# Linear attention and a two-layer network on one core: a new order table, and 16 warm-up matmuls in place of 22

## The chip, the cores and the metric

The kernel runs on one core of a Trainium2 chip. The metric is the device time of one execution in microseconds (us); the median of three runs of the kernel before is 908.88 us (907.92 to 911.11).

## What is computed

Performer attention for 8 batches, 8 heads, 576 positions and head width 64, with 128 random features, and behind it a network of 512 to 2048 to 512 on all 4608 positions, in float32:

```python
def phi(x):                       # x is q or k, scaled by 64 ** -0.25
    proj = np.einsum('bhsd,md->bhsm', x, omega)
    h = proj - np.sum(x * x, axis=-1, keepdims=True) / 2.0
    h = h - np.max(h, axis=-1, keepdims=True)
    return np.exp(h) / np.sqrt(m)
q_p, k_p = (phi(q_s), phi(k_s))
kv = np.einsum('bhsm,bhsd->bhmd', k_p, v)
z = np.sum(k_p, axis=2)
num = np.einsum('bhsm,bhmd->bhsd', q_p, kv)
den = np.einsum('bhsm,bhm->bhs', q_p, z)[..., None] + 1e-06
attn = num / den                  # then reshaped to (4608, 512)
h = x @ w_in
out = np.maximum(0.01 * h, h) @ w_out
```

## The kernel before

Positions are worked in nine blocks of 512. For every block the queries become features, the features are multiplied with the sums of their batch (128 x 65 numbers per head), and the block goes through the network. Numbers are split into a high and a low float16 part, so most products are three matmuls. Blocks 0 to 2 use plain products (L1489 up, L1511 down); from block 3 on the product up has Strassen's seven products (L1397), in the last two blocks the product down too (L1308).

**The first stretch**, which the change moves most, runs up to the first L1489 matmul. The features of batches 0 and 1 and of query block 0 are made in float32 from loads of whole heads: L831 loads q or k, L832 squares it on ScalarE, L858 projects it (32 matmuls to a head pair), L865 takes the maximum on VectorE, L886 subtracts it, L889 takes the exponential. For keys L980 sums features times values. For queries L1076 transposes on TensorE, L1079 takes the exponential, L1107 multiplies with the sums, and L1118 to L1121 divide; the result is split, turned by a DMA (L1033) and is the right operand of L1489.

At the same time the weights come in. L653 loads w_in in eight pieces of 1 MB (L655 the same for w_out) into four buffers, fix_big 88 to 91. Each piece is converted from 64-bit words by L667 (ScalarE), L670 (ScalarE) or L672 (VectorE), and L674; a buffer is free for the next piece when its readers are done. L681 sums squares of each piece on TensorE. When the eighth piece is in, L689 takes the maximum of the sums, L583 (two matmul records) spreads it over the partitions into a tile called scratch, and L587 to L597 on VectorE make the power of two by which all of w_in is scaled. Only then can the pieces be split into high and low parts (L547, L549, L700, L545, L555), and only then can L1489 begin.

The scratch tile is a part of the one PSUM bank "mi" into which L980 writes its sums as well:

```python
scratch = lambda: tiles["mi"][0][:, 384:]
```

**What sets the order.** Every piece of work is an operation with a number, one function that issues some instructions. ORDER is a list of all 3183 numbers; the instructions are issued in exactly that order, each on its engine, and ON names for the operations that can run on several engines which one it is. Nothing else decides the order: an engine works off its own part of the list, and so does SP with the DMAs. Waits between engines are put in where the tiles demand it, by the place in the list: an instruction that reads a tile waits for the writers of that tile that stand ahead of it.

Ahead of the list stand WARM_N matmuls on a constant tile (L1562 and the memset at L1570). Where the planner's own model sees a gap on TensorE, between() puts in further such matmuls of no use (L1562 again, on the identity).

```python
busy(tiles["ffn"][-1], WARM_N, blank)
for o in order:
    ...
    if o in fill and fill[o][0].place < len(tiles[fill[o][0].kind]):
        busy(at(fill[o][0]), fill[o][1], constant)
    o.run()
```

Of the kernel before, what the change touches and what calls it, by code (L numbers as in the profile page):

```python
# [62 lines left out]
WARM_N = 22  # L63
# [405 lines left out]
def performer_ffn(ctx: ExitStack, tc, qT, kT, qn, kn, vn, omT, eye, w_in, w_out, out):  # L469
# [1089 lines left out]
    def busy(bank, n, of):  # L1559

        for _ in range(n):
            nc.tensor.matmul(bank[:, :FILL_N], of[:, :P], of[:, :FILL_N], start=True, stop=True, skip_group_check=True)  # L1562
# [5 lines left out]
    with tc.manual_schedule():  # L1568
        blank = tiles["p32"][1].rearrange("p g m -> p (g m)").bitcast(F16)[:, :FILL_N]
        nc.gpsimd.memset(blank, 1.0)  # L1570
        busy(tiles["ffn"][-1], WARM_N, blank)
        for o in order:
# [53 lines left out]
```

## Time and profile before

| | |
|---|---|
| median of three runs | 908.88 us |
| the profiled execution's own time | 911.08 us |
| its span, first to last instruction | 909.2 us |
| TensorE (PE) busy | 893.3 us, 98% of the span |
| VectorE (DVE) busy | 739.5 us, 81% |
| ScalarE (ACT) busy | 533.3 us, 59% |
| GpSimd (POOL) busy | 378.3 us, 42% |
| mean granted TensorE clock | 0.996 of full speed |
| DMA | 145.91 MB, mean 160 GB/s |

The profile is one execution. Start times count from the first instruction. In the chain of waits each piece stands with its start, its length and what it was: work on an engine, the issue of a DMA (SPq), a DMA in flight, or "issue". In the timeline, the time in brackets is idle time of the engine before the piece, with what ended it. The granted clock is 1.00 at 2.4 GHz and 0.50 at 1.2 GHz.

### The profile page before, as it was taken

To read this page: it belongs to the slowest core of one execution; us is meant where nothing else is said; L and a number is where in the kernel's file an instruction comes from. 1 tells how busy PE (TensorE), PEld (TensorE's weight loads), DVE (VectorE), ACT (ScalarE), POOL (GpSimd) and SP (SyncE) were. 2 spreads that over 40 slices of the span, in tenths; PEclk is the share of its full clock that TensorE was granted. 3 is DMA by queue.
4 is the path that set the end of the run, shared out by engine and by line. 5 is a ranking of instruction groups with operands and counts; after the bars stand their busy time and mean duration, and the time that the engine had idled before them with its cause. 6 is when DMAs were issued, how large, how long until landed. Compare 5 with 4: busy or idle time off the path is not lost.

```text
span 909.2 us, 20952 instructions
## 1 busy us (share of the span) xinstructions
PE 893.3 (98%) x8513; PEld 609.6 (67%) x8513; DVE 739.5 (81%) x1372; ACT 533.3 (59%) x869; POOL 378.3 (42%) x325
## 2 busy tenths in 40 slices
PE   8989999999999999999999999999999999999998
PEld 6886645555555445587558855785578647888887
DVE  5978998778889887979999988889878996965644
ACT  5977778456563465577638874676544643542540
POOL 0141463325344543435623624566455614342511
PEclk9989999999999999999999999999999999999999
DMA  8968359464465669896889978497858744532401
GB/s 335 381 206 225 69 131 192 103 178 107 85 139 159 141 166 229 171 252 161 166 174 229 184 182 175 128 239 146 175 106 221 145 104 100 175 74 73 146 1 47
DMA packets 258784, 145.91 MB, mean 160 GB/s; under 512 B 191360, under 2 KB 238720, under 8 KB 257664
## 3 DMA queue, kind: packets, MB, share of 16 engines
q1 hardware_dynamic: 258688, 144.58, 66.1%
q8 instruction: 66, 1.08, 0.5%
q14 instruction: 30, 0.25, 0.1%
HBM read 81.36 MB, written 16.78 MB: 108 GB/s over the span
## 4 chain that ended last, share of the span: by engine, by line
PE 77%; DVE 15%; DMA 3%; ACT 2%; issue 1%; SPq 1%; DVEq 0%; ACTq 0%
PE fixps_ffn L1511 26%; PE fixps_ffn L1397 19%; PE fixps_ffn L1489 8%; PE lateps_ffn L1397 4%; PE attps_pj L779 4%; PE fixps_ffn L1308 4%; PE lateps_ffn L1308 4%; PE attps_mi L980 1%; DMA fix_row<-qT 1%; DVE proj_st L786 1%; PE attps_mi L1100 1%; DMA fix_big<-w_in 1%; DVE fix_big L555 1%; DVE fix_wt L674 1%; PE attps_mi L1102 1%
## 5 line engine op out<-in xcount | busy, mean ns | idle before, releaser
L1511 PE MATMUL fixps_ffn<-fix_wt,fix_big 128*128 128x512 f16 x1344 | 301.8, 379 | 0.0
L1511 PEld LDWEIGHTS <-fix_big 128*128 128x128 f16 x1344 | 127.1, 98 | 144.8
L1397 PEld LDWEIGHTS <-fix_wt 128*128 128x128 f16 x2016 | 194.6, 98 | 25.6 <-issue 0.5
L1397 PE MATMUL fixps_ffn<-fix_xt,fix_wt 128*128 128x256 f16 x1656 | 190.0, 273 | 0.2 <-DVE fix_row L545 0.2
L555 POOL TENSOR_TENSOR fix_big<-fix_row,fix_big 128x512 f16<-128x512 f32 x82 | 103.0, 1264 | 127.3 <-ACT fix_big L549 86.8
L1489 PE MATMUL fixps_ffn<-fix_xt,fix_wt 128*128 128x512 f16 x576 | 128.5, 379 | 0.0
L1489 PEld LDWEIGHTS <-fix_wt 128*128 128x128 f16 x576 | 54.9, 98 | 63.4
L808 ACT ACTIVATE att_p<-att_p,shift 128x1024 f32<-128x1024 f32 x52 | 59.4, 1142 | 57.3 <-DVE att_p L805 57.2
L555 POOL TENSOR_TENSOR att_ph<-att_p,att_ph 128x1024 f16<-128x1024 f32 x27 | 58.4, 2165 | 74.7 <-ACT att_ph L549 54.3
L786 DVE TENSOR_REDUCE proj_st<-attps_pj 128x8 f32<-128x1024 f32 (+1 forms) x68 | 72.8, 1074 | 11.1 <-PE attps_pj L779 10.8
L549 ACT ACTIVATE fix_big<-fix_row 128x512 f16<-128x512 f32 x108 | 65.7, 625 | 4.1 <-POOL fix_row L1150 1.7
L805 DVE SCALAR_TENSOR_TENSOR att_p<-attps_pj,proj_sc,proj_st 128x1024 f32<-128x1024 f32 x52 | 66.2, 1275 | 1.2
L763 DVE SCALAR_TENSOR_TENSOR proj_z<-proj_nat,proj_sc,proj_z 128x512 f16<-128x512 f32 (+1 forms) x52 | 47.7, 920 | 6.0 <-ACT proj_z L549 5.7
L779 PEld LDWEIGHTS <-proj_t 64*128 64x128 f16 x1416 | 39.7, 94 | 18.5 <-issue 16.9
L1412 DVE TENSOR_TENSOR fix_row<-fix_row,fixps_ffn 128x512 f32<-128x512 f32 x56 | 38.0, 681 | 16.8 <-PE fixps_ffn L1397 13.9
L1420 ACT ACTIVATE fix_row<-fix_row 128x512 f32<-128x512 f32 x69 | 42.6, 622 | 14.1 <-DVE fix_row L1412 14.1
L779 PE MATMUL attps_pj<-om,proj_t 64*128 64x128 f16 x1416 | 50.7, 217 | 0.0
L549 ACT ACTIVATE att_ph<-att_p 128x1024 f16<-128x1024 f32 x46 | 48.2, 1050 | 2.6 <-PE attps_mi L994 1.3
L549 ACT ACTIVATE fix_row<-fixps_ffn 128x512 f32<-128x512 f32 x47 | 27.8, 591 | 34.3 <-PE fixps_ffn L1397 20.5
L555 DVE TENSOR_TENSOR fix_big<-fix_row,fix_big 128x512 f16<-128x512 f32 x57 | 44.0, 775 | 3.6 <-ACT fix_big L549 3.4
L1494 ACT ACTIVATE fix_row<-fixps_ffn 128x512 f32<-128x512 f32 x48 | 28.0, 594 | 31.7 <-PE fixps_ffn L1489 27.4
L739 ACT ACTIVATE proj_z<-proj_nat 128x512 f32<-128x512 f32 (+1 forms) x56 | 36.0, 644 | 16.8 <-DMA proj_nat<-qn 11.2
(251 smaller groups left out, 1746.2 us busy)
## 6 DMA issues: line engine op xcount, KB each, us to landing
fix_wt<-w1s SPq DMA_DIRECT2D x38, 512.0 KB, 4.6
fix_wt<-w1s SPq DMA_DIRECT2D x38, 384.0 KB, 4.2
fix_v<-vn SPq DMA_DIRECT2D x16, 650.0 KB, 5.8
fix_big<-w_in SPq DMA_DIRECT2D x8, 1024.0 KB, 10.8
fix_big<-w_out SPq DMA_DIRECT2D x8, 1024.0 KB, 7.0
proj_nat<-qn SPq DMA_DIRECT2D x32, 256.0 KB, 3.4
out<-fix_row SPq DMA_DIRECT2D x32, 256.0 KB, 2.8
w1s<-fix_y SPq DMA_DIRECT2D x32, 128.0 KB, 2.5
```

The lines of the kernel that those rows point to most:

```text
L549: ("ACT", act(n, int(pointer)), lambda: nc.scalar.activation(dst(), src(), AF.Copy, scale=1.0 if scale is None else value()), False),
L555: o = ways([(e, c, lambda g=g: g.tensor_tensor(dst(), a(), b(), op=ALU.subtract), True) for e, c, g in (("POOL", pool_(n), nc.gpsimd), ("D ...
L763: op("DVE", stt(n) + 0.15, lambda: nc.vector.scalar_tensor_tensor(zl(), heads(), up(), zh(), op0=ALU.mult, op1=ALU.subtract), port=True, r ...
L779: nc.tensor.matmul(at(pj)[:, 512 * h + c * M:512 * h + (c + 1) * M], at(self.t)[r, 2 * (c0 + c) + x, :], om[r, w, :], start=(x + w == 0), ...
L786: op("DVE", dve(n * M), lambda: nc.vector.tensor_reduce(row(0), pv(), axis=AX.X, op=ALU.max), r=[pj], w=[st], prio=prio)
L805: op("DVE", dve(n * M), lambda: nc.vector.scalar_tensor_tensor(p(), pv(), down(), row(2).rearrange("p (g o) -> p g o", o=1).broadcast_to([ ...
L808: op("ACT", act(n * M, 1), lambda: nc.scalar.activation(flat(p()), flat(p()), AF.Exp, bias=shift), w=[p32], r=["ones"], prio=prio)
L1308: nc.tensor.matmul(o, ga(gp, f, 1)[:, 0, P * t:P * t + P], w(f, wp), start=(first and place + f % 2 + t + gp + wp == 0), stop=(place == 3 ...
L1397: nc.tensor.matmul(o, unit(at(wb[c]), u)[:, wp, P * a:P * a + P], mixes[j, c][n][1](xp), start=(first and a == 0 and i == 0), stop=(a == 1 ...
L1420: op("ACT", act(512), lambda: nc.scalar.activation(at(g), at(src), AF.Prelu, scale=H_DOWN_D if finish else H_DOWN_S, alpha=0.01), r=[src], ...
L1489: nc.tensor.matmul(at(ph), wk[wp][:, c:c + P], xt[:, xp, :], start=(k + wp + xp == 0), stop=(k == KT - 1 and wp == 1))
L1511: nc.tensor.matmul(at(po), part(f, gp)[:, t * P:(t + 1) * P], wf[wp], start=(n == 0 and f % 4 == 0 and gp == wp), stop=(n == 3 and f % 4 = ...
```

## The change

WARM_N goes from 22 to 16. ORDER, with the same 3183 operations, is another list, and ON gives 389 operations another engine: 108 go from GpSimd to VectorE, 101 from VectorE to GpSimd, 90 from ScalarE to VectorE and 90 from VectorE to ScalarE. No operation is added or left out; the useless matmuls that between() puts in become 72 in place of 61, since they follow from the list (59 in place of 52 ahead of the first L1489, 13 in place of 9 just behind its first products).

```diff
-WARM_N = 22
+WARM_N = 16
...
 ORDER = [
-    21, 0, 15, 30, 8, 7, 1, 131, 136, 41, 141, 59, 474, 22, 16, 2, 23, 3, 24, 27, 17, 25, 18, 4, 31, 10, 28, 26, 19,
...
 ON = {
...
     "POOL": [
-        40, 57, 75, 94, 111, 129, 178, 181, 189, 192, 242, 247, 271, 283, 291, 295, 299, 307, 311, 315, 319, 323, 361,
...
+        40, 57, 75, 111, 129, 178, 181, 189, 192, 242, 266, 275, 279, 287, 291, 295, 299, 303, 307, 311, 315, 323,
...
```

**SP, the first loads.** proj_nat and fix_row 92 to 95 are heads of q and k, fix_v 108 the values of batch 0, 109 those of batch 1 (650 KB to a row, two where it says x2), fix_big the 1 MB pieces of weights. Before:

```order
L831 DMA proj_nat_178<-kT 128x512
L902 DMA fix_v_108<-vn 128x1300 x2
L609 DMA ident<-eye 128x128
L653 DMA fix_big_88<-w_in 128x2048
L653 DMA fix_big_89<-w_in 128x2048
L831 DMA fix_row_93<-qT 128x512
L653 DMA fix_big_90<-w_in 128x2048
L831 DMA fix_row_94<-qT 128x512
L902 DMA fix_v_109<-vn 128x1300 x2
L653 DMA fix_big_91<-w_in 128x2048
```

Now:

```order
L831 DMA proj_nat_178<-kT 128x512
L609 DMA ident<-eye 128x128
L831 DMA fix_row_93<-qT 128x512
L902 DMA fix_v_108<-vn 128x1300
L831 DMA fix_row_94<-qT 128x512
L902 DMA fix_v_108<-vn 128x1300
L653 DMA fix_big_88<-w_in 128x2048
L653 DMA fix_big_89<-w_in 128x2048
L653 DMA fix_big_90<-w_in 128x2048
L831 DMA proj_nat_177<-kT 128x512
L653 DMA fix_big_91<-w_in 128x2048
```

The identity and the two query heads moved ahead of the weights; of the two halves of fix_v 109 one now stands between the sixth and the seventh piece of w_in and the other behind all eight, so that 650 KB less stand ahead of the eighth piece.

**PE, around the L583 matmul of w_in.** attps_mi 173 is the bank "mi", of which scratch is a part; fix_v and att_ph, fix_row are values and features of batch 1's sums (20 matmuls in four rows). Before:

```order
L858 MATMUL attps_pj_172<-fix_xt_98,fix_row_94 128x128 x2
L583 MATMUL attps_mi_173<-ident,mx_w_131 128x128
L980 MATMUL attps_mi_173<-fix_v_108,att_ph_161 128x65 x4
L980 MATMUL attps_mi_173<-fix_v_108,fix_row_97 128x65
L980 MATMUL attps_mi_173<-fix_v_108,att_ph_161 128x65 x4
L980 MATMUL attps_mi_173<-fix_v_108,fix_row_96 128x65
L1107 MATMUL fixps_ffn_113<-fix_kv_81,att_qp_164 128x65 x4
L980 MATMUL attps_mi_173<-fix_v_108,att_ph_162 128x65 x4
L980 MATMUL attps_mi_173<-fix_v_108,fix_row_97 128x65
```

Now:

```order
L858 MATMUL attps_pj_172<-fix_xt_98,fix_row_94 128x128 x2
L1107 MATMUL fixps_ffn_115<-fix_kv_81,att_qp_164 128x65 x4
L583 MATMUL attps_mi_173<-ident,mx_w_131 128x128
L980 MATMUL attps_mi_173<-fix_v_108,att_ph_161 128x65 x4
L980 MATMUL attps_mi_173<-fix_v_108,fix_row_96 128x65
L980 MATMUL attps_mi_173<-fix_v_108,att_ph_161 128x65 x4
L980 MATMUL attps_mi_173<-fix_v_108,fix_row_97 128x65
L1107 MATMUL fixps_ffn_114<-fix_kv_81,att_qp_164 128x65 x4
L980 MATMUL attps_mi_173<-fix_v_108,att_ph_162 128x65 x4
```

One L1107 group moved ahead of L583. What the rows don't show is the place in the list of VectorE's L587, which reads scratch: before it stood behind both groups of L980, now it stands behind the first and ahead of the second. On PE the two L1076 groups that came next, one before and one behind the next L858 group, now both stand behind that L858 group; and on VectorE one more operation, an L547 that takes 128x256 numbers out of "mi", stands between L587 and the L886 that later L1076 groups wait for.

**SP, the first transposed query features of block 1.** L1067 turns the high and the low part of a head pair's features; att_qp 163 is the first head pair, 164 the second. Before:

```order
L736 DMA proj_nat_178<-qn 128x4x128
L1067 DMA_TRANSPOSE att_qp_163<-att_ph_161 128x8x128 x2
L736 DMA proj_nat_177<-qn 128x4x128
L1067 DMA_TRANSPOSE att_qp_164<-att_ph_162 128x8x128 x2
L765 DMA_TRANSPOSE proj_t_181<-proj_z_180 128x8x128
```

Now:

```order
L736 DMA proj_nat_178<-qn 128x4x128
L1067 DMA_TRANSPOSE att_qp_163<-att_ph_161 128x8x128
L1067 DMA_TRANSPOSE att_qp_164<-att_ph_162 128x8x128
L1067 DMA_TRANSPOSE att_qp_163<-att_ph_161 128x8x128
L1067 DMA_TRANSPOSE att_qp_164<-att_ph_162 128x8x128
L736 DMA proj_nat_177<-qn 128x4x128
```

The second part of the first pair now stands behind the first part of the second pair.

## Rows read from the trace of the kernel before

**Rows 1.** The page, busy time of the engines.

```profile
PE 893.3 (98%) x8513; PEld 609.6 (67%) x8513; DVE 739.5 (81%) x1372; ACT 533.3 (59%) x869; POOL 378.3 (42%) x325
```

**Rows 2.** Busy time by stretch: up to the first L1489, and from there on.

```profile
0.00:72.10 72.10, 64.26 (x693) 58.20 (x694) 52.16 (x94) 53.81 (x70) 13.66 (x18) 0.95 0.86 305
72.10:905.00 832.90, 829.06 (x7822) 551.43 (x7819) 686.47 (x1278) 479.51 (x799) 364.62 (x307) 1.00 0.65 148
```

**Rows 3.** The chain of waits: start, length (us), what.

```profile
6.50 12.17 DMA fix_row<-qT
...
29.61 9.32 DMA fix_big<-w_in
...
43.12 1.99 PE attps_pj L858 x32
45.10 0.42 PE attps_mi L583 x2
45.52 2.18 PE attps_mi L980 x20
47.70 0.89 PE fixps_ffn L1107 x8
48.59 2.25 PE attps_mi L980 x20
...
63.66 3.72 PE attps_pj L858 x32
67.38 2.51 PE fixps_ffn L1107 x16
...
72.12 2.59 PE fixps_ffn L1489 x12
```

**Rows 4.** VectorE's timeline: start, length, what, idle time ahead of it.

```profile
22.54 0.68 DVE L672 TENSOR_SCALAR fix_wt<-fix_big 128x1024 uint32<-128x1024 uint32 x1
...
50.87 0.29 DVE L587 TENSOR_REDUCE pow_w<-attps_mi 128x1 f32<-128x128 f32 x1 [4.49 <-PE attps_mi L980]
...
57.73 0.42 DVE L1121 TENSOR_TENSOR fix_y<-fixps_ffn,att_r 128x256 f32<-128x256 f32 x1
...
59.32 1.22 DVE L886 TENSOR_TENSOR att_p<-attps_pj,proj_st 128x1024 f32<-128x1024 f32 x1
```

**Rows 5.** Busy time by stretch around 60 us; behind the counts granted clock, DMA share, GB/s.

```profile
50.00:62.50 12.50, 9.69 (x108) 8.65 (x107) 11.22 (x24) 10.55 (x15) 5.34 (x3) 0.97 0.88 293
62.50:67.50 5.00, 4.96 (x37) 4.40 (x38) 3.14 (x6) 4.93 (x7) 5.00 (x4) 0.50 0.77 148
67.50:72.10 4.60, 4.60 (x37) 4.56 (x38) 3.56 (x9) 2.93 (x3) 0.41 (x1) 0.89 1.12 283
```

**Rows 6.** The same view while the loads run; the last number is GB/s.

```profile
12.50:37.50 25.00, 22.89 (x281) 21.24 (x278) 21.27 (x40) 20.32 (x28) 0.00 (x0) 1.00 1.02 414
```

**Rows 7.** SP's timeline, three issues of w_in pieces that took 5.90 us.

```profile
24.04 5.90 SPq L653 DMA_DIRECT2D fix_big<-w_in  x3
```

**Rows 8.** PE's timeline.

```profile
1.10 4.88 PE L1562 MATMUL fixps_ffn<-att_p 128*128 128x256 f16 x22 [1.10 <-POOL att_p L1570]
5.90 2.62 PE L858 MATMUL attps_pj<-fix_xt,fix_row 64*128 64x128 f32 x32
...
53.10 0.66 PE L1076 MATMUL fixps_ffn<-ident,att_p 128*128 128x128 f32 x4 [1.38 <-DVE att_p L886]
...
75.01 1.14 PE L1562 MATMUL attps_pj<-ident 128*128 128x256 f16 x9
```

**Rows 9.** The page's costliest groups: busy us, mean ns of one.

```profile
L808 ACT ACTIVATE att_p<-att_p,shift 128x1024 f32<-128x1024 f32 x52 | 59.4, 1142 | 57.3 <-DVE att_p L805 57.2
...
L786 DVE TENSOR_REDUCE proj_st<-attps_pj 128x8 f32<-128x1024 f32 (+1 forms) x68 | 72.8, 1074 | 11.1 <-PE attps_pj L779 10.8
...
L805 DVE SCALAR_TENSOR_TENSOR att_p<-attps_pj,proj_sc,proj_st 128x1024 f32<-128x1024 f32 x52 | 66.2, 1275 | 1.2
...
L549 ACT ACTIVATE att_ph<-att_p 128x1024 f16<-128x1024 f32 x46 | 48.2, 1050 | 2.6 <-PE attps_mi L994 1.3
```

433 rows, old and new, of tables (ON, ORDER) are left out of this document.

## The prediction

> **What bounds the kernel now.** I read the page first: PE is busy for 893.3 us of a span of 909.2 [rows 1], so a change of order can only give back what is left, 15.9 us, and what runs at half clock. Then the busy times by stretch, to see where that lies [rows 2]. Behind the first L1489 matmul PE idles for 3.84 us of 832.90 (832.90 - 829.06) at a clock of 1.00; ahead of it for 7.84 us of 72.10, at a mean clock of 0.95. The rest lies at the ends. So the time is the start of L1489, 72.12 us [rows 3], and a packed 837 us behind it. The chain of waits for the start reads, in order of time: a query load that took 12.17 us from its issue at 6.50, since values and two pieces of weights stood ahead of it in the queue; the eighth piece of w_in, issued at 29.61 and landed at 38.93; some conversion; L583; two groups of L980 with an L1107 between them [rows 3]; and then VectorE's L587, which had been idle for 4.49 us and was let go by L980 [rows 4]. L587 needs only L583's result, which was there at 45.52; it waited until 50.87 because both L980 groups write the same bank and stand ahead of it in the list. After it VectorE works almost without a break (11.22 us of 12.50) while PE waits (9.69 us busy) [rows 5], until the L886 that ends at 60.54 [rows 4]. Then comes a stretch of PE at half clock: 0.50 for 62.50 to 67.50 [rows 5].
>
> **The change part by part.** All times are those of the profiled execution: 911.08 us with a span of 909.2. It lies 2.20 above the median of 908.88; I take the difference that the change makes from its rows and put it on the median.
>
> 1. *Loads.* From 12.5 to 37.5 us the queue moves 414 GB/s without a gap (DMA share 1.02) [rows 6]. Of what stood ahead of the eighth w_in piece, 650 KB (666 kB) now stand behind it: 666 / 414 = 1.6 us earlier, at 37.3. This is the end of the range for the good. The other end: the pieces 5 to 8 must wait for a free buffer, as three of them did on SP for 5.90 us [rows 7]. The buffer of the seventh is released by an L672 that ran at 22.54 [rows 4] and that now stands on VectorE behind divisions of the first query head. From its issue the eighth piece had 9.32 us [rows 3], so a release up to some 7 us later than 29.6 is hidden; if it were 10 us later, the last two megabytes would start some 10 us late and take 2 x 1049 / 414 = 5.1 us, a landing at about 40, 1.1 later than now. I take -1.6: the query loads that the divisions need are moved ahead of the weights too, and their 12.17 us shrink.
>
> 2. *L1107 ahead of L583.* One group of 8 is 0.89 us [rows 3]: +0.9.
>
> 3. *L587 no longer behind the second L980 group.* Between L583 and L587 now stands one group of L980 (2.18) on PE; the L1107 (0.89) and the second L980 (2.25) come later [rows 3]: -3.14. With 1 to 3, L587 starts at 50.87 - 1.6 + 0.9 - 3.1 = 47.0 in place of 50.87.
>
> 4. *VectorE from L587 to L886.* From 50.87 to 60.54 this is nearly solid work [rows 4, 5]; now it is the same operations in another sequence and one L547 of 128 x 256 numbers more; the nearest row is an L1121 of that size, 0.42 [rows 4]: +0.4. L886 then ends near 57.1. PE has waits to lose here as well: L1076 waited 1.38 us for L886 [rows 8]; now an L858 group of 1.99 [rows 3] stands ahead of it and covers that.
>
> 5. *The clock.* The half-clock stretch costs (1 - 0.97) x 12.50 + 0.50 x 5.00 + (1 - 0.89) x 4.60 = 3.4 us [rows 5], all on the path: behind L886 PE works without a break up to L1489, and there L858 took 3.72 in place of 1.99 and 16 L1107 matmuls 2.51 in place of 1.78 [rows 3]. It began after a stretch in which PE was busy 9.69 of 12.50 us [rows 5]. In the new order most of that idle time is gone, as VectorE is 3.5 us ahead and the transposes stand later. I take the whole 3.4 back; the other end is 0. The clock gate has a rule in the Trainium skill, in "TensorE: Matmul & The Clock Gate", section "HAM oscillation — how this bites in real kernels": PE keeps its full clock so long as no long idle gap interrupts it. By that rule gaps such as the 1.38 us of that stretch [rows 8] cost no clock, the half-clock stretch would have a cause that the new order leaves alone, and the sum would be without step 5: -3.0, 905.9 us. By the rows, in which the clock fell when small gaps had added up, it is -6.4. I go by the rows.
>
> 6. *Warm-up.* 22 matmuls took 4.88 us, 0.222 each [rows 8]: six fewer are 1.3 us. The first L858 came at 5.90 directly behind them [rows 8], so it can start up to 1.3 earlier. That is hidden: PE waits for loads afterwards, and the path runs through the eighth piece. I take 0; bounds -1.3 and, if the clock rises later for it, +1.3, hidden by the same loads. If the loads were no longer the bound, the whole 1.3 would count.
>
> 7. *Filling matmuls.* 13 in place of 9 behind the first L1489; 9 took about 1 us [rows 8]: +0.4. The 59 in place of 52 ahead of it stand in gaps of the loads: 0.
>
> 8. *The 389 operations on another engine, and the packed part.* DVE's and ACT's sums hardly move, as the exchanges are 108 against 101 and 90 against 90. What it does to the 3.84 us of PE idle [rows 2] the trace of before cannot show: between -1.9 (half of them go) and +6.4 (rival 2). I take 0, since before the packed part leaves the engines other than PE free for 17% and more of it (686.47 of 832.90 for VectorE) [rows 2].
>
> Sum: -1.6 + 0.9 - 3.1 + 0.4 - 3.4 + 0.4 = -6.4 us. L1489 starts at about 65.4, and 908.88 - 6.4 = **902.5 us**.
>
> **The rivals.**
>
> *1. The clock falls again.* Everything as above, but PE still waits ahead of the later L1076. From L583, now at 45.10 - 1.6 + 0.9 = 44.4, its work is 0.42 + 2.18 + 0.89 + 2.25 + 1.99 [rows 3], two L1076 of 0.66 [rows 8], another L858 and another L1107 of 1.99 and 0.89 [rows 3]: 11.9 us, to 56.3, and L886 ends at 57.1. That leaves a gap of 0.8 us, and more where ScalarE's exponentials come late. For it speaks that small gaps were enough before; against it, that PE idled 2.81 us of those 12.50 [rows 5], three times as much. The time is 902.5 + 3.4 = 905.9.
>
> *2. The gain before L1489 is given back behind it.* The packed part was idle for 3.84 us in 832.90 [rows 2]; a list with a new sequence of everything can have more. It decides from 6.4 us more, 10.2 in all, and the time is then 908.9, no change. Against it: VectorE, ScalarE and GpSimd have the same sums as before.
>
> *3. Slower: SP's transposes of block 1.* The second part of the first head pair's features now waits in SP's queue for the first part of the second pair. That part exists only after the second pair's maximum (L786 1.07), subtraction (L805 1.28), exponential (L808 1.14) and high part (L549 1.05) [rows 9], together 4.5 us, if they come after those of the first pair with nothing between. Where PE has no other work left, the num product waits that long, and a wait of that length can take the clock with it, 3.4 more by step 5: 7.9 us in all, and the time is 902.5 + 7.9 = 910.4. With the fall of the clock it decides from a wait of 3.0 us. Against it: PE has L1489 products to do meanwhile, and both pairs' projections stand close together.
>
> **How the numbers follow.** A measurement of this kernel can tell about 0.3%, 2.7 us, from no change: faster means below 906.15, slower above 911.6. My chances: forecast 0.55, rival 1 0.20, rival 2 0.15, rival 3 0.10. Rival 1 at 905.9 lies at the border, so half of it counts as faster, half as the same; nearly all of rival 2 is the same, with a little in either direction; of rival 3 six parts in ten are slower. Faster: 0.55 + 0.10 + 0.01 = 0.66; slower: 0.06 + 0.01 = 0.07; same: the rest, 0.27. The range starts at 898.5: the forecast with half the packed idle gone (-1.9), a warm-up that counts (-1.3) and rounding. It goes up to 909.8, over the late loads (+2.7), rival 1 and rival 2, and leaves out most of rival 3 and a little below. The likeliest case alone reaches from 899 to 905.2 (late loads).
>
> **What would show it.** In the changed profile L587 for w_in should start near 47 and show an idle time of 2 to 3 us before it, ended by L980; the eighth w_in piece should land near 37.3; the granted clock should be 1.00 from 12.5 us on, with no 0.50 stretch between 50 and 70; the first L1489 should start near 65.4. PE's idle time behind it should be 2 to 6 us. The query load that took 12.17 us should take 4 to 6. If L1489 starts near 69 with a half-clock stretch ahead of it, rival 1 holds; if it starts near 65 and the span is still 905 or more, rival 2 or 3, told apart by whether PE's waits for att_qp exceed 3 us in one place. The prediction is wrong if L587 still waits until 50 or later, or if the eighth piece lands after 39.

## The result, and the profile after

The changed kernel takes **915.06 us** (914.12 to 917.76, five runs) against 909.53 (907.92 to 911.11) for the kernel before, measured beside it. The ratio is 1.0066, with an interval of 1.0044 to 1.0088: slower by 0.7%. The forecast was 902.5, faster. The profiled execution took 914.36 with a span of 912.4, that is 3.2 more than the span of before.

The page, busy time of the engines after [rows 1]:

```profile
PE 892.0 (98%) x8518; PEld 607.5 (67%) x8518; DVE 757.4 (83%) x1379; ACT 536.2 (59%) x869; POOL 368.9 (40%) x318
```

Busy time by stretch after [rows 2, 5, 6]:

```profile
0.00:72.10 72.10, 67.01 (x745) 59.68 (x745) 60.04 (x102) 57.00 (x71) 14.81 (x19) 1.00 0.85 304
72.10:905.00 832.90, 821.56 (x7746) 545.00 (x7745) 696.28 (x1276) 478.49 (x797) 354.13 (x299) 1.00 0.65 148
12.50:37.50 25.00, 24.91 (x301) 23.01 (x300) 23.36 (x41) 20.68 (x25) 0.00 (x0) 1.00 1.02 413
50.00:62.50 12.50, 10.14 (x123) 9.07 (x121) 12.14 (x19) 10.07 (x15) 7.46 (x5) 1.00 0.51 174
62.50:67.50 5.00, 5.00 (x39) 3.98 (x38) 4.66 (x11) 4.74 (x6) 4.41 (x4) 1.00 0.62 207
```

PE's and VectorE's timelines after [rows 3, 4, 8]:

```profile
50.93 0.66 PE L1076 MATMUL fixps_ffn<-ident,att_p 128*128 128x128 f32 x4
53.83 0.66 PE L1076 MATMUL fixps_ffn<-ident,att_p 128*128 128x128 f32 x4 [2.25 <-DVE fix_y L1121]
...
65.59 2.75 PE L1489 MATMUL fixps_ffn<-fix_xt,fix_wt 128*128 128x512 f16 x12
68.18 1.58 PE L1562 MATMUL fixps_ffn<-ident 128*128 128x256 f16 x13
```

```profile
45.92 0.29 DVE L587 TENSOR_REDUCE pow_w<-attps_mi 128x1 f32<-128x128 f32 x1 [2.26 <-PE attps_mi L980]
...
53.37 0.41 DVE L1121 TENSOR_TENSOR fix_y<-fixps_ffn,att_r 128x256 f32<-128x256 f32 x1
```

The first stretch came out almost as forecast: L1489 starts at 65.59 us instead of 72.12, the half-clock stretch before it is gone (1.00 from 62.5 to 67.5, where before had 0.50), and L587 starts at 45.92 after 2.26 us of idle time. It is behind L1489 that the time went. PE's idle time there is 832.90 - 821.56 = 11.34 us, where before had 3.84 [rows 2]. The longest of PE's waits from 72 to 905 us (in total, times, longest); first those of before, then those of after:

```profile
PE attps_mi L1102 <- DMA att_qp<-att_ph: 1.2, 2, 0.8
PE attps_pj L858 <- ACT att_p L802: 0.9, 1, 0.9
PE attps_mi L1100 <- DVE fix_x L1121: 0.6, 1, 0.6
```

```profile
PE fixps_ffn L1511 <- DVE fix_row L1412: 1.7, 1, 1.7
PE attps_mi L1102 <- DMA att_qp<-att_ph: 1.6, 2, 1.1
PE attps_pj L779 <- DMA proj_t<-proj_z: 1.5, 3, 0.6
PE fixps_ffn L1397 <- DMA fix_xt<-fix_xn: 1.4, 1, 1.4
PE attps_mi L992 <- DVE proj_st L791: 1.0, 1, 1.0
```

No wait is long; there are more of them, for VectorE and for transposes by DMA.

**The lag table.** To see where a kernel gains or loses, the two traces are laid side by side at equal work of PE: each matmul counts with the spacing that its kind has when nothing waits (0.216 us for a 128x512 product of L1489 or L1511, 0.109 for L1397, and so on; filling matmuls count zero), and the lag is the difference in time at which the same sum is reached. The reference is the profiled execution of before (911.08, some 2 us above its median), so that much of a gain belongs to the reference. A minus means earlier than before. The columns are times in the trace of before.

```
                          79   111   189   204   360   391   437   468   593   623   881
after                   -5.9  -5.6  -6.7  -5.3  -6.4  -2.1  -0.5  +1.1  +1.5  +3.1  +3.5
after, 22 warm-ups      -5.8  -5.5  -6.6  -5.6  -6.9  -4.8  -1.7  -1.0  -0.6  +1.4  +1.9
new to 347, then old    -5.7  -5.4  -0.2  -0.2  -0.7  -0.7  -0.4  -0.4  -0.4  -0.4  -0.1
old to 347, then new    -1.1  -1.1  -2.2  +0.8  -0.5  +0.9  +3.0  +4.2  +4.6  +7.4  +8.1
new to 510, then old    -4.8  -4.5  -6.0  -6.0  -7.0  -7.0  -6.6  -6.6  -6.6  -6.6  -6.7
new to 1014, then old   -4.6  -4.3  -5.4  -1.1  -1.9  -1.9  -1.9  -1.9  -1.2  -1.2  -1.1
read of L587 alone      -5.1  -5.1  -5.2  -5.2  -5.8  -5.8  -5.8  -5.8  -5.0  -5.0  -5.0
```

After is 6 us ahead from 80 to 360 us and then gives up 10 us, 4 of them between 375 and 391.

**The place at 384 us.** SP's waits and timeline of after, and busy time by stretch:

```profile
SPq L736 <- DVE proj_z L763: 5.4, 1, 5.4
```

```profile
373.51 0.39 SPq L736 DMA_DIRECT2D proj_nat<-qn  x1
...
376.21 5.61 SPq L1033 DMA_TRANSPOSE fix_xt<-fix_xn  x2
```

```profile
380.00:384.00 4.00, 1.94 (x42) 1.51 (x41) 3.88 (x4) 2.40 (x5) 0.00 (x0) 1.00 1.12 248
384.00:388.00 4.00, 4.00 (x40) 2.90 (x39) 3.97 (x7) 1.43 (x3) 2.12 (x1) 0.57 1.09 183
```

SP waits 5.4 us to issue a query load (L736, operation 1501), because VectorE still reads its buffer. Behind it in SP's queue stand the two L1033 transposes that L1397 needs. PE idles for 2.06 of 4.00 us, and then the granted clock is 0.57 for 4 us, another 0.43 x 4 = 1.7 us.

**The place at 421 us.** Timelines of VectorE, GpSimd and PE of after:

```profile
418.65 1.12 DVE L791 SCALAR_TENSOR_TENSOR proj_st<-proj_st,proj_sc,proj_sq 128x8 f32<-128x8 f32 x1
419.80 2.04 DVE L796 SCALAR_TENSOR_TENSOR proj_st<-proj_sq,proj_st 128x8 f32<-128x8 f32 x1
...
422.13 0.68 DVE L1412 TENSOR_TENSOR fix_row<-fix_row,fixps_ffn 128x512 f32<-128x512 f32 x1
```

```profile
417.60 2.14 POOL L555 TENSOR_TENSOR fix_big<-fix_row,fix_big 128x512 f16<-128x512 f32 x1
419.70 2.12 POOL L555 TENSOR_TENSOR att_ph<-att_p,att_ph 128x1024 f16<-128x1024 f32 x1
```

```profile
422.86 1.46 PE L1511 MATMUL fixps_ffn<-fix_wt,fix_big 128*128 128x512 f16 x6 [1.71 <-DVE fix_row L1412]
```

Two operations on 128 x 8 numbers take 1.12 and 2.04 us. They end at 419.77 and 421.84, and GpSimd's two operations end at 419.74 and 421.82: each of VectorE's ended with the one of GpSimd that had started ahead of it. L1412 stands behind them, and PE waits 1.71 us for L1412. The groups of these two lines, before and after (total, mean ns), first before:

```profile
L791 DVE SCALAR_TENSOR_TENSOR proj_st<-proj_st,proj_sc,proj_sq 128x8 f32<-128x8 f32 (+1 forms) x68 | 27.5, 404 | 0.4
L796 DVE SCALAR_TENSOR_TENSOR proj_st<-proj_sq,proj_st 128x8 f32<-128x8 f32 x52 | 15.2, 293 | 1.8
```

```profile
L791 DVE SCALAR_TENSOR_TENSOR proj_st<-proj_st,proj_sc,proj_sq 128x8 f32<-128x8 f32 (+1 forms) x68 | 34.3, 504 | 0.5
L796 DVE SCALAR_TENSOR_TENSOR proj_st<-proj_sq,proj_st 128x8 f32<-128x8 f32 x52 | 21.0, 403 | 1.8
```

The same operations take 12.6 us more in all (34.3 + 21.0 against 27.5 + 15.2), since more of them fall beside GpSimd's: of the 120, 32 take over 0.5 us in after and 19 in before, and every one of these ends 0.02 to 0.03 us behind a GpSimd operation that had started ahead of it. VectorE's busy time as a whole grew by 17.9 us, from 739.5 [rows 1] to 757.4.

### The profile page after: what moved, and what is told of

The parts are those of the page before. It is cut to its first block, busy times and chain, and to the rows that moved or that the text cites. A ratio compares the mean times of both kernels' runs of the same rounds, so it can differ in the third digit from the quotient of the medians.

```text
span 912.4 us, 20980 instructions
## 1 busy us (share of the span) xinstructions
PE 892.0 (98%) x8518; PEld 607.5 (67%) x8518; DVE 757.4 (83%) x1379; ACT 536.2 (59%) x869; POOL 368.9 (40%) x318
## 4 chain that ended last, share of the span: by engine, by line
PE 73%; DVE 17%; DMA 4%; issue 2%; ACT 2%; POOL 1%; SPq 1%; DVEq 0%; ACTq 0%; POOLq 0%
PE fixps_ffn L1511 24%; PE fixps_ffn L1397 14%; PE fixps_ffn L1489 8%; PE lateps_ffn L1397 5%; PE lateps_ffn L1308 5%; PE attps_pj L779 4%; PE fixps_ffn L1308 3%; PE attps_mi L980 2%; DMA att_qp<-att_ph 1%; DVE proj_z L763 1%; PE attps_pj L858 1%; DVE fix_big L555 1%; DVE fix_wt L674 1%; DVE att_p L805 1%; PE attps_mi L1100 1%
## 5 line engine op out<-in xcount | busy, mean ns | idle before, releaser
L1511 PE MATMUL fixps_ffn<-fix_wt,fix_big 128*128 128x512 f16 x1344 | 301.6, 379 | 1.7 <-DVE fix_row L1412 1.7
L1511 PEld LDWEIGHTS <-fix_big 128*128 128x128 f16 x1344 | 127.2, 98 | 147.3 <-issue 1.9
L1397 PEld LDWEIGHTS <-fix_wt 128*128 128x128 f16 x2016 | 194.7, 98 | 28.5 <-issue 2.6
L1397 PE MATMUL fixps_ffn<-fix_xt,fix_wt 128*128 128x256 f16 x1608 | 186.5, 273 | 2.0 <-DMA fix_xt<-fix_xn 1.4
L555 POOL TENSOR_TENSOR fix_big<-fix_row,fix_big 128x512 f16<-128x512 f32 x86 | 107.9, 1265 | 137.7 <-ACT fix_big L549 72.8
L1489 PE MATMUL fixps_ffn<-fix_xt,fix_wt 128*128 128x512 f16 x576 | 128.6, 379 | 0.0
L555 POOL TENSOR_TENSOR att_ph<-att_p,att_ph 128x1024 f16<-128x1024 f32 x33 | 71.5, 2169 | 78.9 <-ACT att_ph L549 62.6
L1489 PEld LDWEIGHTS <-fix_wt 128*128 128x128 f16 x576 | 54.9, 98 | 63.0
L549 ACT ACTIVATE fix_big<-fix_row 128x512 f16<-128x512 f32 x111 | 67.5, 623 | 6.1 <-DVE fix_row L1150 4.1
L1412 DVE TENSOR_TENSOR fix_row<-fix_row,fixps_ffn 128x512 f32<-128x512 f32 x57 | 38.6, 682 | 19.1 <-PE fixps_ffn L1397 15.7
L763 DVE SCALAR_TENSOR_TENSOR proj_z<-proj_nat,proj_sc,proj_z 128x512 f16<-128x512 f32 (+1 forms) x52 | 51.0, 983 | 2.9 <-ACT proj_z L549 2.7
L549 ACT ACTIVATE att_ph<-att_p 128x1024 f16<-128x1024 f32 x49 | 51.2, 1049 | 3.5 <-PE attps_mi L980 2.9
L555 DVE TENSOR_TENSOR fix_big<-fix_row,fix_big 128x512 f16<-128x512 f32 x56 | 45.2, 809 | 5.7 <-ACT fix_big L549 5.6
L549 ACT ACTIVATE fix_row<-fixps_ffn 128x512 f32<-128x512 f32 x45 | 26.7, 593 | 38.8 <-PE fixps_ffn L1397 31.9
L1397 PE MATMUL lateps_ffn<-fix_xt,fix_wt 128*128 128x256 f16 x408 | 47.8, 273 | 0.0
```

Of the source, the lines that this page charges most:

```text
L549: ("ACT", act(n, int(pointer)), lambda: nc.scalar.activation(dst(), src(), AF.Copy, scale=1.0 if scale is None else value()), False),
L555: o = ways([(e, c, lambda g=g: g.tensor_tensor(dst(), a(), b(), op=ALU.subtract), True) for e, c, g in (("POOL", pool_(n), nc.gpsimd), ("D ...
L763: op("DVE", stt(n) + 0.15, lambda: nc.vector.scalar_tensor_tensor(zl(), heads(), up(), zh(), op0=ALU.mult, op1=ALU.subtract), port=True, r ...
L1397: nc.tensor.matmul(o, unit(at(wb[c]), u)[:, wp, P * a:P * a + P], mixes[j, c][n][1](xp), start=(first and a == 0 and i == 0), stop=(a == 1 ...
L1489: nc.tensor.matmul(at(ph), wk[wp][:, c:c + P], xt[:, xp, :], start=(k + wp + xp == 0), stop=(k == KT - 1 and wp == 1))
L1511: nc.tensor.matmul(at(po), part(f, gp)[:, t * P:(t + 1) * P], wf[wp], start=(n == 0 and f % 4 == 0 and gp == wp), stop=(n == 3 and f % 4 = ...
```

## The experiments

Kernels with longer tables have their lines 6 to 8 further down: L590 or L591 there is L583, L1084 is L1076. Before was measured beside each set; its medians were 908.8 to 909.4, with single runs from 905 to 917. The ratio is to before in the same set, with its interval; it comes from the single runs, so it is not always the quotient of the two medians. The edits of the lists are written in short.

**The two halves apart.** NEW and OLD are the two tables; each operation runs on the engine of the table from which its place comes.

```diff
-ORDER = NEW
+ORDER = NEW[:347] + [n for n in OLD if n not in NEW[:347]]
```

> The first 347 operations of the new list with their new engines and 16 warm-up matmuls, and behind them all others in the order and on the engines of the list before. Theory A (the new list gains about 6 us ahead of the first L1489 and loses about 10 us in the packed part, independently of each other): L1489 starts near 66, PE idles behind it for about 4 us as before, and the time is 3 to 6 us below the kernel before (904 to 906.5 against 909.5). Rival B (the loss is the price of the head: work that arrives 6 us earlier collides with loads and buffers later on): the time is above the kernel before, near 913 to 915, with waits of PE behind 350 us.

Measured: 911.12, ratio 1.0022 (1.0006 to 1.0038).

```diff
-ORDER = NEW
+ORDER = OLD[:347] + [n for n in NEW if n not in OLD[:347]]
-WARM_N = 16
+WARM_N = 22
```

> The mirror image: the first 347 operations and 22 warm-up matmuls of the kernel before, and behind them the new list and its engines. Theory A: L1489 starts near 72 as before, PE idles behind it for some 11 us, and the time is 9 to 10 us above the kernel before (918 to 920). Rival B: no more than 3 us above the kernel before (912 or less), since the head that causes the loss is gone.

Measured: 919.16, ratio 1.0114 (1.0079 to 1.0150). The new list behind entry 347 loses 9 us by itself (-1.1 to +8.1 in the lag table), as it does in after (-5.9 to +3.5). The first half failed to show its gain: the lag is -5.4 at 111 us and -0.2 at 189. PE's timeline there:

```profile
117.33 0.49 PE L590 MATMUL attps_mi<-ident,mx_v 128*128 128x128 f32 x2 [2.82 <-DVE fix_kv L1015]
117.66 1.76 PE L1569 MATMUL attps_pj<-ident 128*128 128x256 f16 x9
```

It is the joint: L583 waits 2.82 us for VectorE, the clock is at half for 3.4 us behind it (118.0 to 121.4), and the planner has put filling matmuls there. So it was done once more without the 13 fillers behind the joint:

```diff
-    fill = between(order)
+    fill = {o: f for o, f in between(order).items() if order.index(o) < 347}
```

> The first 347 entries of the new list and the rest of the old one, as in the run that took 911.1, without the 13 filling matmuls at 118 to 137 us (1.4 us, some of them at half clock). Theory (what was lost at the joint is a wait of 2.8 us for VectorE, the clock's fall behind it and these fillers): 909, between 908 and 910, the wait and the fall still there. Rival (the fillers keep the clock up and cost nothing): 911 to 912.

Measured: 909.35, ratio 1.0011 (0.9997 to 1.0025). By the ratios that is some 1 us less than with them, with intervals that overlap. The wait there was 1.4, without a fall of the clock, and behind the joint the lag stays: -2.5 at 189 us, -2.2 at the end. A splice has a cost at its joint, and the joint has to be chosen.

**The splice further on.**

```diff
+ORDER = NEW[:1014] + [n for n in OLD if n not in NEW[:1014]]
```

> The first 1014 entries of the new list with the new engines (some 295 us of the span), the rest of the old list with the old engines; 16 warm-ups. Theory A (the new first stretch gains some 6 us, the new list's packed part loses some 9, nearly all of it behind 360 us): 903.5, between 902 and 905.5, PE's lag against before about -6 from 80 us to the end. Rival (a lead is given back whatever list follows, since loads and VectorE set the pace of the packed part, as behind the joint of the run with 347 entries): 908 to 911, with the lag back at 0 within some 100 us of the joint.

Measured: 909.34, ratio 0.9992 (0.9968 to 1.0017). Busy time by stretch:

```profile
190.00:197.70 7.70, 5.76 (x33) 2.45 (x31) 7.63 (x12) 3.58 (x7) 5.82 (x5) 1.00 1.07 177
197.70:201.10 3.40, 3.08 (x16) 1.42 (x17) 2.54 (x7) 0.60 (x1) 0.94 (x1) 0.51 1.06 259
```

The lead goes in one place, 190 to 201 us: PE idles 1.94 us for query transposes (L1067) and the clock falls. In after's trace the first of these transposes is issued at 187.7 us, behind a v load and a weight load, and lands at 194.5, 6.8 us later (before: 199.5 to 203.1, 3.6); the same place cost 1.3 there. So the splice was put ahead of it:

```diff
+ORDER = NEW[:510] + [n for n in OLD if n not in NEW[:510]]
```

> The first 510 entries of the new list with the new engines (some 146 us of the span, so past the new first stretch and ahead of the query transposes near 190 us), the rest of the old list with the old engines; 16 warm-ups. Theory A (the new first stretch gains 6 us, and the places near 195, 384, 421 and 460 us, which all lie behind entry 510 of the new list, give it back): 904, between 902.5 and 905.5, with a lag against before of -5 to -6.5 us that stays to the end. Rival (the packed part gives a lead back whatever list follows): 908 to 911, with the lag back near 0 behind 200 us.

Measured: **904.48**, ratio 0.9948 (0.9923 to 0.9972): faster than both kernels. PE's waits from 72 us on are down to

```profile
PE attps_mi L591 <- DVE mx_w L697: 0.8, 1, 0.8
```

and smaller ones. The packed part keeps a lead when its list is the old one. The loss is the new list, with its engines, behind entry 510.

**Order or engines.** 389 operations change engine. Behind entry 347 all got their old engine back, with the new order:

```diff
-ON = NEW_ON
+ON = {operation: (NEW_ON if operation in NEW[:347] else OLD_ON)}
```

> The new list whole; behind its entry 347 every operation on the engine that it had before. Theory E1 (the loss of the packed part comes from the moves between VectorE, ScalarE and GpSimd): 907 to 910, the stalls behind 380 us gone. Theory E2 (it comes from the order of the entries, SP's above all): 914 to 917, with the stall of L1397 near 384 us still there.

Measured: 984.83, ratio 1.0831 (1.0795 to 1.0868). That decides for neither theory: PE has 635 matmuls more, fillers that the planner put in where it foresaw waits. Without them behind entry 347:

> The new list whole with the old engines behind entry 347, as in the run that took 985, but without the filling matmuls behind entry 347: the planner had put 635 of them there, since it foresaw waits (69 us at 0.109 each). Theory E2 (the order makes the waits, the engines little): 915 to 922. Theory E1 (the engine moves make them, the old engines take them away): 906 to 910. If the old engines fit the new order worse than the new ones: over 922.

Measured: 950.40, ratio 1.0456 (1.0429 to 1.0484). PE's line of the page, with and without those fillers:

```profile
PE 959.7 (98%) x9153; PEld 668.6 (68%) x9153; DVE 762.9 (78%) x1373; ACT 533.1 (54%) x868; POOL 377.3 (38%) x325
```

```profile
PE 905.2 (95%) x8518; PEld 613.2 (65%) x8518; DVE 759.1 (80%) x1373; ACT 532.5 (56%) x868; POOL 378.4 (40%) x325
```

So to take the engine moves back doesn't mend the new order, it makes it 35 us worse. The old order with the new engines was not run. Order and engines are one plan, and half of it can't be judged alone: how the loss divides between them stays open.

**Mending the new list.**

```diff
-..., 1501, 1699, ..., 1193, ..., 1195, ..., 1196, ..., 1701, ...
+..., 1193, 1501, ..., 1195, 1196, 1699, 1701, ...
```

> The changed kernel with one place of SP's queue in another order: the two L1033 transposes of block 4 ahead of a query load that waits for its buffer and of a load of values (and the L912 that reads these behind them). Theory C (at 383.8 us PE waited for these transposes for 1.4 us because they stood in SP's queue behind the load, and the wait took the clock with it, 3.4 us of half speed costing half of that or more): the wait of L1397 for fix_xt and the half-clock stretch at 384 us are gone, and the time is about 3 us below the changed kernel (912 against 915). Rival: the transposes were late for the work that makes their input; then the wait stays and the time is that of the changed kernel, 915.

Measured: 922.66, ratio 1.0139 (1.0113 to 1.0166). The edit made a worse wait, as VectorE's timeline and PE's show:

```profile
384.61 1.49 DVE L920 TENSOR_REDUCE mx_v<-fix_v 128x1 f32<-128x1280 f32 x1 [7.77 <-DMA fix_v<-vn]
```

```profile
389.82 1.47 PE L787 MATMUL attps_pj<-om,proj_t 64*128 64x128 f16 x24 [5.49 <-DVE att_p L813]
```

The v loads that it put later are awaited by VectorE, which stood still for 7.77 us. Next, operation 1193 alone:

```diff
-..., 1501, 1699, 1463, 1193, ...
+..., 1193, 1501, 1699, 1463, ...
```

> The new list with one entry moved: operation 1193 (an L1033 transpose of block 4) ahead of operation 1501 (an L736 query load that waits for its buffer) on SP; the v loads stay where they are, unlike the run that moved them too. Theory C (the wait of 1.4 us of L1397 at 384 us and the clock's fall behind it come from this transpose standing behind 1501): 912, between 910.5 and 913.5, no half-clock stretch near 385 us. Rival (the other transposes' turn on the queue or the engines sets it): 914.5 to 916.

Measured: 916.07, ratio 1.0065 (1.0038 to 1.0092). At its place it did what was meant: between 375 and 391 us the loss is 1.6, not 4.0, with no half clock. But in the profiled execution the place at 195 us, where the list is after's, took 4.0 in place of 1.3 (1.9 of waits and half clock from 196 us for 3.4), and the median did not fall. Six moves at once:

```diff
+1193 ahead of 1501
+999, 421 behind 779, 780, 805
+2274, 1972 behind 2211, 2212
+1510 behind 1291
```

> The new list whole, with six entries moved: 1193 (L1033 transpose) ahead of 1501 (query load); the loads 999 (v) and 421 (L1164) behind the query transposes 779, 780 and 805; the weight loads 2274 and 1972 behind the query transposes 2211 and 2212; VectorE's 1510 (the small operations of L797's helper) behind 1291 (L1412). Theory N (the loss of the packed part is the sum of these named waits: 1.3 near 195 us, 4.0 near 384, 1.9 near 421, 1.3 near 611): 907, between 905.5 and 909. Rival (there is no slack in the new list's packed part: what is mended at one place is lost at another): 912.5 to 917.

Measured: 914.33, ratio 1.0058 (1.0028 to 1.0087). Up to 593 us the lag is 4.4 better than after's (-2.9 against +1.5); then PE waits for one of the weight loads that were moved, and the clock falls:

```profile
609.08 3.17 PE L1405 MATMUL fixps_ffn<-fix_xt,fix_wt 128*128 128x256 f16 x14 [2.27 <-DMA fix_wt<-w1s]
```

Without the third line of that diff:

> The new list whole with four of the six moves of the earlier mending: 1193 ahead of 1501; 999 and 421 behind 780 and 805; 1510 behind 1291. The weight loads 2274 and 1972 stay where the new list has them (in the run with all six, PE's lag was 4.3 us better than the new kernel's up to 592 us, and the product behind those two loads then waited 2.4 us at 607 with a half-clock stretch, 4 us lost). Theory N (the waits are places that can be mended one by one, and moving those two loads was itself the mistake): 911, between 909.5 and 912.5, with the lag at 592 us kept to 640 but for some 1.3 us. Rival (the packed part has no slack: any mending is lost elsewhere): 913 to 917.

Measured: 912.77, ratio 1.0040 (1.0028 to 1.0053), between the two ranges. PE's timeline of this run:

```profile
382.48 0.34 PE L787 MATMUL attps_pj<-om,proj_t 64*128 64x128 f16 x6 [0.74 <-DMA proj_t<-proj_z]
...
425.70 1.47 PE L1405 MATMUL fixps_ffn<-fix_xt,fix_wt 128*128 128x256 f16 x12 [0.49 <-DVE fix_row L1420]
```

Where after waited 1.4 and 1.7 us there are 0.74 and 0.49. And the same without its 9 fillers behind entry 347:

> The new list with the four moves (1193, 999, 421, 1510), without the 9 filling matmuls that the planner had put behind entry 347 (some 1.0 us at 381 and 435). Theory N with fillers as the part that hid it: 911.5, between 910.5 and 912.3. If the fillers lay in waits that are there anyway: 912.8, as with them.

Measured: 912.13, ratio 1.0037 (1.0020 to 1.0053), which can't be told from 912.77. So waits can be mended one by one, but other waits remain or take their place: four moves meant for some 7 us give 2 to 3 by the ratios, and the intervals of these still overlap with that of after (1.0044 to 1.0088). From 80 us to the end the first of the two kernels loses 6.9 us in its profile (-5.3 to +1.6) and the second 6.0 (-1.8 to +4.2), not 9.4.

**The read of L587 alone**, on the old list: operation 173 (L587 to L597) directly behind 172 (L583), ahead of both L980 groups (83, 90).

```diff
-172, 83, 68, 90, 71, 98, 173, 99,
+172, 173, 83, 68, 90, 71, 98, 99,
```

> The kernel before with one operation moved: the read of w_in's maximum (L587 to L597 on VectorE) directly behind its L583 in the list, so that it waits for neither group of L980. Theory D (step 3 of the prediction: both groups write the bank that L587 reads, and the wait for them sits on the path to the first L1489): L587 starts near 45.6 in place of 50.9, L1489 3 to 5 us earlier than 72.1, and if the half-clock stretch goes as well up to 7; the time is 2 to 5 us below the kernel before. Rival E (VectorE's wait was hidden; the loads and PE's own work set the start): L1489 within 1 us of 72 and the time unchanged.

Measured: 906.07, ratio 0.9957 (0.9941 to 0.9973). VectorE's timeline, and busy time by stretch:

```profile
45.39 0.29 DVE L593 TENSOR_REDUCE pow_w<-attps_mi 128x1 f32<-128x128 f32 x1 [0.67 <-PE attps_mi L589]
```

```profile
62.50:67.50 5.00, 5.00 (x42) 4.41 (x43) 4.45 (x10) 4.79 (x5) 1.71 (x3) 1.00 1.13 266
```

L587 (here L593) starts 5.5 us earlier, released by L583 and no longer by L980, and the half-clock stretch is gone from this trace. One moved entry gives 3.3 of the 4.5 us that the best splice gives.

**The loads and the warm-ups.** The old list with that read, the new order of the first loads and 16 warm-ups, then the same with 22:

```diff
+1, 41, 7, 59, 8 behind 30; 473 behind 113; 475 behind 82; 477 behind 484
+173 behind 172
```

> The old list and engines with the new order of the first loads, with operation 173 directly behind 172, and with 16 warm-ups. Theory D plus step 1 (the loads are worth 1.6 to 4 us beside the 3.3 of the read): 904, between 902 and 905. Rival (what the loads gain ahead of 25 us is waited out at the next load, so that the read alone counts): 906, between 905.3 and 907.

Measured: 906.98, ratio 0.9975 (0.9951 to 0.9999).

> The old list and engines with the new order of the first loads, with operation 173 directly behind 172, and with 22 warm-ups (as the earlier run with 16, and nothing else changed). If the warm-ups count for the clock in the first 25 us (the run with 16 had 6.8 us at half clock there, the one with the read alone and 22 had 3.4): 904, between 902.5 and 905.5. If they do not: 906.5, between 905.5 and 908.

Measured: 908.23, ratio 0.9996 (0.9967 to 1.0024). Both miss their better case: on the old list the loads add nothing to the read alone that can be seen in the time, and 22 warm-ups are no better than 16. (In the trace of the second the lag is -6.4 at 79 us, 1.3 better than with the read alone; 3.0 of it go at 147 us, where L1102 waits 1.7 us and the clock falls. In the first the clock is at half from 19.5 to 26.3 us. Ten of its twelve runs have a mean clock of 0.994 to 0.996 and took 906.7 to 910.7 us; the two with 0.999 took 903.8 and 903.9. So the loads may be worth what was expected where the clock holds, but two runs don't show it.) With the new list:

> The new list whole, with 22 warm-ups in place of 16. Step 6 of the forecast (the warm-ups cost nothing, since they end ahead of the first load's landing): 915, as with 16, between 914 and 916. Rival (fewer or more of them change when the clock is granted or delay the first product): over 1.5 us away from 915 on either side.

Measured: 914.11, ratio 1.0054 (1.0029 to 1.0080), the same as with 16. This trace is the best witness against the clock as the main cause: it has no half-clock stretch ahead of 910 us, and still loses from -5.8 to +1.9. PE's timeline of it:

```profile
382.61 1.14 PE L1405 MATMUL fixps_ffn<-fix_xt,fix_wt 128*128 128x256 f16 x9 [1.46 <-DMA fix_xt<-fix_xn]
...
388.61 0.20 PE L1108 MATMUL attps_mi<-fix_kv,att_qp 128*128 128x65 f16 x1 [1.36 <-DMA att_qp<-att_ph]
```

**What is left of the first stretch.** On the best splice, the L1121 operations ahead of the scalings of the weights:

```diff
-72, 176, 90, 91, 73, ...
+72, 73, 176, 90, 91, ...
-69, 174, 180, ..., 116, 70,
+69, 70, 174, 180, ..., 116,
```

> The run with the first 510 entries of the new list, with two entries moved: 73 (L1121) directly behind 72, and 70 (L1121) directly behind 69, both L1120, on VectorE, so ahead of the weight scalings 174, 180, 176 and 175. Theory (the 2.25 us for which PE's L1076 waits at 51 us for L1121, which stands behind some 4 us of scalings on VectorE, go): 902.3, between 901 and 903.5. Rival (the scalings, later by as much, are awaited next, by L1489): 904 to 905, as without the edit.

Measured: 905.57, ratio 0.9960 (0.9945 to 0.9974), no gain. The wait for L1121 is gone, and its size stands at the next L1076:

```profile
56.98 1.97 PE L1084 MATMUL fixps_ffn<-ident,att_p 128*128 128x128 f32 x8 [2.27 <-DVE att_p L894]
```

VectorE works without a break there; to move an operation ahead moves another one back.

## Why the prediction was wrong, step by step

**Steps 1 to 5 and 7 were right in sum.** Together they said that L1489 would start near 65.4; in after's trace it started at 65.59, 6.5 us earlier. The splice at entry 510 shows 4.5 us of that in the time (904.48); before's trace, from which the 6.5 are taken, lay 2.2 above its median. The sum was met in part by luck, since steps 1 to 3 gave more and step 4 less than forecast.

- *Step 1 (loads, -1.6).* The last piece of w_in landed at 36.2 in place of 38.93, so -2.7, by SP's rows of after (issued at 27.1, 9.1 to its landing):

```profile
L653 SPq DMA_DIRECT2D fix_big<-w_in x2: 328/328/328, 25.6 to 27.1; - x2
...
DMA to landing us min/median/max: 8.1/8.6/9.1
```

- *Steps 2 and 3 (L587 near 47.0).* 45.92, and the idle time ahead of it 2.26 in place of 4.49. The read alone shows step 3 by itself.
- *Step 4 (VectorE to L1489, L1076 covered).* Failed: the same operations did not take the same time, and L1076 was not covered. One L547 took 2.56 us, where the other eight of its size on w_in and w_out in both traces took 0.72 to 0.75. GpSimd's L555 had started 0.12 us ahead of it:

```profile
50.49 2.56 DVE L547 TENSOR_SCALAR fix_wt<-fix_wt,pow_w 128x1024 f32<-128x1024 f32 x1
```

```profile
50.37 2.13 POOL L555 TENSOR_TENSOR fix_wt<-fix_wt,fix_wt 128x1024 f16<-128x1024 f32 x1 [5.16 <-DVE att_r L1118]
```

With the two L1121 moved ahead it started at 50.84 us, beside the same L555, and took 2.11. In after L1121 stands behind it on VectorE, and PE's L1076 waited 2.25 us for L1121. From L587 to L1489 it took 19.7 us, where the forecast had 18.4.
- *Step 5 (clock, -3.4).* Right for these two traces, but not a matter of the order alone. Both profiled kernels with the old first stretch (before; old to 347, then new) run at half clock for 6.8 us from 60 to 62 us on. Ahead of that PE had waited 1.38 us [rows 8] and, in before's timeline, 1.25:

```profile
60.60 0.66 PE L1076 MATMUL fixps_ffn<-ident,att_p 128*128 128x128 f32 x4 [1.25 <-DVE att_p L886]
```

So the Trainium skill's reading in "TensorE: Matmul & The Clock Gate", section "HAM oscillation — how this bites in real kernels", which left the stretch out of the sum, did not hold here: no single gap there was longer than some 1.4 us [rows 8]. With the new first stretch left as it is, 13 kernels were profiled, and in all of them PE waits 2.25 us for L1121 at 51 or 52 us. Eight keep the full clock behind it, after among them. Five fall to half from 53 or 54 us on, four of them for 3.4 us and one for 10.2, and their L1489 starts at 66.6 to 69.7 in place of 64.8 to 66.4. The splice at 510 is one of the five:

```profile
54.20:57.60 3.40, 3.40 (x33) 3.40 (x32) 3.10 (x4) 2.15 (x4) 0.69 (x1) 0.50 0.02 6
```

So rival 1, to which I gave 0.20, is what some executions do, and that after's trace kept its clock there is in part luck.
- *Step 6 (warm-ups, 0).* Right as far as can be told: 914.11 with 22, 915.06 with 16.

**Step 8 failed.** It put the packed part at 0, because the engines' sums would hardly change and VectorE had 17% free. What happened is rival 2, which I gave 0.15 and priced at 908.9, the lead just given back; it "decides from 6.4 us more". By the sign set for it, L1489 near 65 and no wait for att_qp over 3 us (the longest is 1.1), it is rival 2 and not rival 3. PE's idle time there grew by 7.5 us (11.34 against 3.84) and the clock cost 1.7, some 9 in all, so the time went past no change to 0.7% slower. The end of step 8's range, +6.4, was too low. Its premise did not hold either: VectorE's sum grew by 17.9 us, 12.6 of them in L791 and L796 beside GpSimd's work, though the numbers of operations moved each way are nearly equal. And the step rested on the wrong quantity. A packed list runs on slack at single places: a transpose that stands behind a blocked load in SP's queue, an L1412 behind two small operations. Sums of engines do not show these, and the shown difference of the two lists would have had to be followed queue by queue. Rival 3 (SP's transposes of block 1) did not happen; transposes that came late out of SP's queue did, at 195 and 384 us.

**Still open.** That the loss lies behind entry 510 of the new plan is shown, and the places at 195, 384 and 421 us are shown. How the loss divides between the order and the engines is not. Of some 9 us the four moves took back 2 to 3 by the ratios; the other 6 lie in small waits that were not taken apart.

## What to carry to other kernels

Look for a result that sits in a shared bank: to read it before the next writers of the bank was worth 3.3 us of 909 with one moved entry. When a whole order is searched anew, splice the old and the new list at points where both have done the same work and measure each half, with the joint's own cost and the planner's fillers in mind; the good half may be all that is wanted. In a packed part count the slack of each queue at its tightest places, not the engines' sums. And look at what runs on GpSimd beside each VectorE operation: the same L547 took 0.74 us alone and 2.56 beside L555.

## What the runs showed of the hardware

VectorE's operations on 128 x 8 numbers take 0.17 or 0.22 us (the medians of L796 and L791) and up to 2.6 us when GpSimd works: they then end within 0.03 us of GpSimd's operation (419.77 and 419.74; 421.84 and 421.82; the same in all 51 cases of over 0.5 us in the two traces). The Trainium skill, "SBUF — State Buffer", section "SBUF: two separate sides", says that VectorE (with two SBUF inputs) and GpSimd share a pair of ports under an exclusive lock that the one that starts first holds for its whole instruction; by that rule a small operation costs what is left of GpSimd's, and these rows agree.

The clock does not fall by rule at a given wait. Behind the same wait of 2.25 us at 51 or 52 us it fell in five of 13 profiled kernels and held in eight. At 384 us after had 2.06 us of idle time in 4 and then half clock; with 22 warm-ups the same list waited 1.46 and 1.36 us there and kept its clock, and the execution ran without a fall up to 910 us. A stretch at half clock lasted 3.4, 6.8 or 10.2 us here and costs up to half of that, so a profile with one more or less differs by that from the median.
